# Value products in four and five matmuls, an early split of q and k, and a new order around the softmax

## The chip, the cores and the metric

One Trainium2 chip, one core of it. The metric is the device time of one execution in microseconds (us). A core's engines each work through their own queue and wait for each other by semaphores: PE (TensorE, matrix products), DVE (VectorE) and ACT (ScalarE) for elementwise work, SP and POOL, which here mostly start transfers.

## What is computed

Local and global attention (8 batches, 8 heads, 512 local and 32 global tokens, head size 64; a local query sees the local keys within 32 places and all global keys, a global query sees all keys), and a feed-forward block on the result, all in fp32:

```python
s_g = scale * np.matmul(q_g, k_all.transpose(0, 1, 3, 2))
out_g = np.matmul(sm(s_g), v_all)
s_ll = scale * np.matmul(q_l, k_l.transpose(0, 1, 3, 2))
...
s_ll = np.where(mask, s_ll, -1000000000.0)
s_lg = scale * np.matmul(q_l, k_g.transpose(0, 1, 3, 2))
s_l = np.concatenate([s_lg, s_ll], axis=-1)
a_l = sm(s_l)
out_l = np.matmul(a_l, np.concatenate([v_g, v_l], axis=2))
return np.concatenate([out_g, out_l], axis=2).astype(np.float32)
...
x = np.ascontiguousarray(attn_out.transpose(0, 2, 1, 3)).reshape(B * S, H * D)
...
h = np.maximum(x @ w_in, 0.0)
return (h * h @ w_out).astype(np.float32)
```

`sm` is the softmax with 1e-9 added to the sum; `k_all` and `v_all` are the global and the local ones together.

## The kernel before

The local tokens are cut into 16 blocks of 256, and each block with each of the 8 heads is one "head" t, 128 in all. The main loop (line 589) runs a step t for each head, with step m = t - 9 of the feed-forward block beside it (17 blocks of 256 tokens, 8 steps each: `gemm1` makes 256 hidden columns, `act1` and `act2` square the Relu and split it, `gemm2` adds to the output). The first 16 heads run in plain fp32 while the weights arrive. From then on numbers are split into a high part that PE reads fast (F32R) and a remainder, and a product is the sum of high x high, remainder x high and high x remainder. The change is about this part.

In step t, `transposes` brings the probabilities of head t-1 to the bank pt, `scores` makes those of head t, `pt_split` (ACT casts) and `pt_rest` (DVE remainders) split pt, `softmax1` to `softmax3` are the maxima (DVE), the exponentials with their sums (ACT) and the scaling by the reciprocals for two tiles of 128 queries (DVE), `av` multiplies head t-1's probabilities by its values into the bank xa, `x_evac` brings that to x_h (ACT) and x_l (DVE), which `gemm1` reads, and `split_head` splits the packed q, k and v of head t+1 (raw). The global queries ride along: `g_scores` and `g_evac` collect their scores, and per 16 heads two groups go through a table of jobs (line 654): `g_soft`, `g_exp`, `g_norm`, `g_tr` (transposes), `g_rest` (remainders), and for two pairs each `g_split_v`, `g_av` (products gxo, in the bank xa as well) and `g_x`.

From step 17 on the three engines work in the order in which the code is written (`FREE`, line 591); nothing is reordered. A tile of a pool with one buffer (xa, pt, r) is reused only when its readers are done. The profile gives nearly all instructions line 52, the helper that records them, so they are told apart by tiles.

Of the kernel before, what the change touches and what calls it, by code (L numbers as in the profile page):

```python
# [32 lines left out]
SQ = (2, 3, 4, 5, 14, 15)  # L33
# [25 lines left out]
def attention_moe(  # L59
# [65 lines left out]
    def split_head(t):  # L125

        hd = heads[t]
        raw = hd["raw"]
# [8 lines left out]
        hd["hi"], hd["lo"] = hi, lo  # L137
# [64 lines left out]
    def pt_split(t):  # L202
        hd = heads[t]
        if plain(t):
            pts = p2.tile([P, 512], F32, tag="gh", name=f"pts{t}")
            ac.copy(pts, pt)
            hd["pts"] = pts
            return
        ph = p1.tile([P, 640], F32R, tag="ph", name=f"ph{t}")
        pl = p1.tile([P, 256], F32R, tag="pl", name=f"pl{t}")  # L210
# [4 lines left out]
        hd["ph"], hd["pl"] = ph, pl  # L215

    def pt_rest(t):
        if plain(t):
            return
        ph, pl = heads[t]["ph"], heads[t]["pl"]  # L220
        ve.tensor_sub(pl, pt[:, :256], f(ph[:, :256]))
        ve.tensor_sub(ph[64:, 256:384], pt[:64, 320:448], f(ph[:64, 256:384]))

        ve.tensor_sub(ph[64:, 384:640], pt[64:, 256:512], f(ph[:64, 384:640]))

    def av(t):
        hd = heads[t]
        c = QC + KC
        if plain(t):

            xa = ps_a.tile([P, HALF], F32, tag="xa", name=f"xa{t}")
            v, pts = hd["raw"][:, c:], hd["pts"]
            mm = [
                (xa, v[:, 0:128], pts[:, 256:512]),
                (xa[:, 0:128], v[:, 64:192], pts[:, 0:128]),
                (xa[:, 128:256], v[:, 128:256], pts[:, 128:256]),
            ]
        else:
# [12 lines left out]

    def x_evac(t):
# [3 lines left out]
        if g == 0:  # L256
            ac.copy(xg[r, h // 2, :], xa)
# [7 lines left out]
    def g_load(t):  # L265
# [7 lines left out]
        if plain(t):  # L273
            qz = p1.tile([P, 512], F32, tag=("ph", "gvl", "gvh", "ph")[t // 4], name=f"qz{t}")
# [43 lines left out]
    def g_split_v(t, pair):  # L318

        gv = state["gv"]  # L320
        gvh = p1.tile([P, 5, P], F32R, tag="gvh", name=f"gvh{t}_{pair}")
        gvl = p1.tile([P, 4, P], F32R, tag="gvl", name=f"gvl{t}_{pair}")
# [3 lines left out]
        state["gvs"] = gvh, gvl  # L326
# [38 lines left out]
    def g_rest(t):  # L365
        (pth, gt), ge = state["gpt"], state["ge"]
        ptl = p1.tile([P, 512], F32R, tag="ptl", name=f"ptl{t}")
        ac.copy(pth[:64, 512:], ge[:64, :])
        ve.tensor_sub(ptl, gt, f(pth[:, :512]))
        ve.tensor_sub(pth[64:, 512:], ge[64:, :], f(pth[:64, 512:]))  # L370
        state["gpt"] = pth, ptl

    def g_av(t, pair):
        (gvh, gvl), (pth, ptl) = state["gvs"], state["gpt"]
        xo = ps_a.tile([64, P], F32, tag="xa", name=f"gxo{t}_{pair}")
        mm = []
        for c in range(4):
            cols = slice(128 * c + 64 * pair, 128 * c + 64 * pair + 64)
            mm += [(pth[:, cols], gvh[:, c, :]), (pth[:, cols], gvl[:, c, :]), (ptl[:, cols], gvh[:, c, :])]
        mm.append((pth[:, 512 + 64 * pair : 576 + 64 * pair], gvh[:, 4, :]))  # L380
        for i, (x, y) in enumerate(mm):
            pe.matmul(xo, x, y, start=i == 0, stop=i == len(mm) - 1)
        xs = p1.tile([64, P], F32, tag="xs", name=f"gxs{t}_{pair}")
        ac.activation(out=xs, in_=xo, func=AF.Copy, scale=state["gst", t][:64, pair : pair + 1])
# [58 lines left out]
    def gemm1(m, j):  # L443
# [12 lines left out]
        for n, (a, b) in enumerate(mm):  # L456
            pe.matmul(hp[:, j, :], a, b, start=n == 0, stop=n == len(mm) - 1)

    def act1(m):
# [4 lines left out]
        if m < 8 or m + LAG < NT + 8 and (m + LAG) % 16 in SQ:  # L464
# [124 lines left out]
    for t in range(NSTEP + LAG + 1):  # L589
# [53 lines left out]
        if t + 1 < NT:  # L643
            split_head(t + 1)
# [7 lines left out]
        if live and t % 4 == 3 and (t // 8) % 2 == 1:  # L652
            d = t if t % 8 == 3 else t + 2
            for at, *job in (
# [12 lines left out]
                (max(d + 6, 17), 1, g_av, 1),  # L667
                (max(d + 7, 18), 3, g_x, 1),
# [102 lines left out]
```

## Time and profile before

| | us |
|---|---|
| median of 3 runs (lowest, highest) | 1068.83 (1068.39, 1069.07) |
| the profiled execution | 1068.82 |
| its span | 1067.0 |

In the lines of the profile shown below, the engines' line gives busy time, share of the span and instructions; a line of a stretch gives, for PE, its weight loads (PEld), DVE, ACT and POOL, the busy time with the count, then the granted PE clock (1.00 is full), the DMA share and GB/s. A line of the chain has start, length and what ran; a line of a timeline has start, length, engine, operation, output and input tiles, and in brackets the idle time before it with who ended it. A group's line ends with total busy time, the mean of one in ns, and the idle time before.

### The profile page before, as it was taken

What the parts mean: (1) busy time and instruction counts of PE and PEld (TensorE: products, weight loads), DVE (VectorE), ACT (ScalarE), POOL (GpSimd) and SP (SyncE); (2) the same over time, 40 slices, a digit from 0 to 9 for tenths busy, and PEclk for the clock granted to TensorE, in tenths of its full rate; (3) what the DMA queues carried; (4) which work ended last, traced back from release to release, by engine and by line L of the source; (5) the groups of instructions that cost most, each with busy time, mean ns of one, the idle gap of its engine ahead of it and who ended that gap; (6) DMA issues with size and microseconds to landing.
All of it is one profiled execution on the core that took longest, in us unless ns stands there. A gap on an engine that the chain in (4) does not pass through costs nothing.

```text
span 1067.0 us, 21142 instructions
## 1 busy us (share of the span) xinstructions
PE 1050.4 (98%) x7568; PEld 941.7 (88%) x7568; DVE 856.3 (80%) x2687; ACT 753.1 (71%) x1901; POOL 3.9 (0%) x14
## 2 busy tenths in 40 slices
PE   7999999999999999999999999999999999999998
PEld 6776889999998989998999989999999989999896
DVE  5698988898888989988888888888888888874321
ACT  5898877778777776778777777777777787774322
POOL 1000000000000000000000000000000000000000
PEclk9999999999999999999999999999999999999999
DMA  9772132223222322222322222223221322201000
GB/s 372 310 263 74 57 106 76 71 80 98 68 89 64 103 65 83 74 91 77 94 71 82 86 72 76 90 66 100 78 89 55 94 86 66 88 29 33 13 20 20
DMA packets 54312, 96.78 MB, mean 91 GB/s; under 512 B 4288, under 2 KB 29376, under 8 KB 54208
## 3 DMA queue, kind: packets, MB, share of 16 engines
q1 hardware_dynamic: 54064, 95.37, 27.2%
q8 instruction: 60, 0.98, 0.4%
q14 instruction: 44, 0.36, 0.1%
q10 hardware_dynamic: 144, 0.07, 0.0%
HBM read 86.51 MB, written 8.91 MB: 89 GB/s over the span
## 4 chain that ended last, share of the span: by engine, by line
PE 87%; ACT 7%; DVE 4%; issue 1%; DMA 0%; ACTq 0%
PE o L52 33%; PE h L52 32%; PE xa L52 7%; PE s L52 6%; PE pt L52 5%; PE gxo L52 2%; PE gs L52 2%; ACT prob L52 1%; DVE prob L52 1%; ACT r L52 1%; ACT ph L52 1%; ACT hi L52 1%; ACT ot L52 1%; PE gt L52 1%; ACT sg L52 0%
## 5 line engine op out<-in xcount | busy, mean ns | idle before, releaser
L52 PE MATMUL h<-x_h,ws 128*128 128x256 f32 x2048 | 388.9, 283 | 0.0
L52 PEld LDWEIGHTS h<-x_h,ws 128*128 128x128 f32 x2048 | 327.0, 191 | 0.5
L52 PE MATMUL o<-ws,gh 128*128 128x512 f32 x1024 | 321.3, 395 | 0.0
L52 PE MATMUL h<-x_l,ws 128*128 128x256 f32 x1024 | 289.1, 282 | 0.1
L52 PEld LDWEIGHTS o<-ws,gh 128*128 128x128 f32 x1024 | 185.5, 188 | 34.6
L52 PE MATMUL o<-ws,gl 128*128 128x512 f32 x512 | 202.6, 396 | 0.0
L52 PEld LDWEIGHTS h<-x_l,ws 128*128 128x128 f32 x1024 | 195.9, 191 | 0.9 <-DVE x_l L52 0.4
L52 ACT CAST ph<-pt 128x256 fp32r<-128x256 f32 x448 | 141.1, 341 | 67.7 <-PE pt L52 60.8
L52 ACT ACTIVATE prob<-prob,st 128x224 f32<-128x224 f32 x270 | 127.8, 475 | 61.2 <-DVE st L52 59.1
L52 ACT ACTIVATE r<-h 128x512 f32<-128x512 f32 x136 | 81.4, 599 | 112.3 <-PE h L52 112.3
L52 PEld LDWEIGHTS o<-ws,gl 128*128 128x128 f32 x512 | 96.2, 188 | 22.7
L52 DVE CUSTOM_DVE_ANT_0 prob<-s,con 128x224 f32<-128x224 f32 x256 | 90.0, 386 | 24.5 <-PE s L52 23.2
L52 DVE TENSOR_TENSOR gl<-r,gh 128x512 fp32r<-128x512 f32 x128 | 87.9, 686 | 23.3 <-ACT gh L52 20.5
L52 ACT CAST hi<-raw 128x864 fp32r<-128x864 f32 x112 | 102.5, 915 | 1.4
L52 DVE TENSOR_TENSOR r<-h,r 128x512 f32<-128x512 f32 x82 | 56.7, 692 | 51.9 <-ACT r L52 50.6
L52 PE MATMUL xa<-ph,hi 128*64 128x128 f32 x448 | 87.3, 238 | 1.6 <-DVE ph L52 1.2
L52 DVE TENSOR_TENSOR hi<-raw,hi 64x352 fp32r<-64x352 f32 x224 | 82.5, 368 | 6.4
L52 ACT CAST gh<-r 128x512 fp32r<-128x512 f32 x128 | 79.1, 618 | 9.1 <-DVE r L52 8.7
L52 DVE TENSOR_TENSOR ph<-pt,ph 64x128 fp32r<-64x128 f32 x224 | 79.6, 355 | 7.0
L52 DVE TENSOR_TENSOR lo<-raw,hi 128x448 fp32r<-128x448 f32 x112 | 69.6, 622 | 15.3 <-ACT hi L52 12.5
L52 PE MATMUL pt<-con,prob 128*128 128x128 f32 (+1 forms) x512 | 78.2, 274 | 0.7 <-ACT prob L52 0.5
L52 DVE TENSOR_SCALAR prob<-prob,st 128x224 f32<-128x224 f32 x242 | 70.7, 334 | 4.1
(80 smaller groups left out, 1572.7 us busy)
## 6 DMA issues: line engine op xcount, KB each, us to landing
raw<-in_pk_dram SPq DMA_DIRECT2D x127, 432.0 KB, 3.2
wr<-in_w_dram SPq DMA_DIRECT2D x32, 512.0 KB, 7.9
gv<-in_vg_dram SPq DMA_DIRECT2D x32, 320.0 KB, 3.3
out_dram<-ot SPq DMA_DIRECT2D x32, 256.0 KB, 2.2
qr<-in_qg_dram SPq DMA_DIRECT2D x31, 64.0 KB, 2.8
out_dram<-ot SPq DMA_DIRECT2D x8, 64.0 KB, 1.7
con<-in_consts_dram SPq DMA_DIRECT2D x2, 224.0 KB, 5.1
raw<-in_pk_dram SPq DMA_DIRECT2D x1, 304.0 KB, 3.2
```

The lines of the kernel that those rows point to most:

```text
L52: r = method(*args, **kwargs)
```

## The change

The parts of v and of the probabilities are laid side by side, so that one product of 128 weight columns makes high x high and the remainder products at once: four matmuls for a local head instead of nine, five for a global pair instead of 13. The pieces then stand in different places of the bank, and DVE adds them (two additions more in `x_evac`, a new `g_add`). q and k get a tile of their own (kq), split before the softmax of the step before; v is split late. `pt_rest` moves ahead of the maxima. The scaling of the second tile, and Relu's square in all steps with heads, go to ACT, the global scores are scaled on ACT ahead of the transposes, and the second half of `gemm1` is cut in two around `av`. `v_g` is packed twice instead of three times, and some tiles take over others' buffers.

```diff
-        hi = p2.tile([P, PK], F32R, tag="hi", name=f"hi{t}")
-        lo = p2.tile([P, QC + 192], F32R, tag="lo", name=f"lo{t}")
-        ac.copy(hi, raw)
-        ve.tensor_sub(lo, raw[:, KC : KC + QC + 192], f(hi[:, KC : KC + QC + 192]))
...
+        kq = p2.tile([P, c + QC], F32R, tag="kq", name=f"kq{t}")
+        ac.copy(kq[:, :c], raw[:, :c])
...
+        ve.tensor_sub(hd["lo"], raw[:, KC : KC + QC], f(hi[:, KC:]))
         ve.tensor_sub(hi[64:, :KC], raw[64:, :KC], f(hi[64:, :KC]))
-        ve.tensor_sub(hi[32:64, PK - 64 :], raw[32:64, PK - 64 :], f(hi[32:64, PK - 64 :]))
...
+        ac.copy(vs[:, :, :64], vr)
+        ve.tensor_sub(vs[:, :, 64:], vr, f(vs[:, :, :64]))
...
+        for u in tiles:
-            if MUL <= t < NPLAIN:
+            if MUL <= t < NPLAIN or t >= NPLAIN and u == 1:
                 ac.activation(out=w_, in_=w_, func=AF.Copy, scale=st[:, u : u + 1])
...
-        ac.copy(ph[:, :256], pt[:, :256])
-        ac.copy(ph[:64, 256:384], pt[:64, 320:448])
-        for r in (0, 32):
-            ac.copy(ph[r : r + 32, 384:640], pt[64:96, 256:512])
+        ac.copy(pb[:, :, 0, :], pt[:, :256].rearrange("p (u n) -> p u n", u=2))
+        ac.copy(ps[:64, 512:640], pt[:64, 320:448])
+        ac.copy(ps[:64, 640:], pt[64:, 256:])
...
+            mm = [(both, vs[2], ps[:, 512:640]), (xb[:, :, 0, :], vs[3], ps[:, 640:])]
+            mm += [(xa[:, 256 * u : 256 * u + 256], vs[u], ps[:, 256 * u : 256 * u + 256]) for u in range(2)]
...
-            ac.copy(x_h[r, g % 2, h // 2, :], xa)
-            ve.tensor_sub(x_l[r, g % 2, h // 2, :], xa, f(x_h[r, g % 2, h // 2, :]))
+            ac.copy(x0, xb[:64, :, 0, :])
+            ve.tensor_sub(xr, xb[:64, :, 0, :], f(x0))
+            ve.tensor_add(xr, xb[:64, :, 1, :], xr)
+            ve.tensor_add(x1, xb[64:, :, 0, :], xr)
...
+        ac.activation(out=s[:, :544], in_=s[:, :544], func=AF.Copy, scale=st[:, 0:1])
+        for o in (544, 576):
+            ac.copy(s[:, o : o + 32], s[:, 512:544])
...
-            mm += [(pth[:, cols], gvh[:, c, :]), (pth[:, cols], gvl[:, c, :]), (ptl[:, cols], gvh[:, c, :])]
+            mm.append((xo, pts[:, o : o + 128], gvs[:, c : c + 6 : 5, :]))
...
+    def g_add(t, pair):
+        xs, xo = state["xs"]
+        ve.tensor_add(xs, xo[:64, 1, :], xs)
+        ve.tensor_add(xs, xo[64:, 0, :], xs)
...
-        if m < 8 or m + LAG < NT + 8 and (m + LAG) % 16 in SQ:
+        if m + LAG < NT:
             ac.activation(out=r, in_=r, func=AF.Square)
...
+        late, split = prev and not plain(t - 1), t + 1 < NT
         if prev:
             pt_split(t - 1)
+            if late:
+                pt_rest(t - 1)
...
+        if split and late:
+            split_kq(t + 1)
         if live:
             softmax1(t)
             softmax2(t)
-        if prev:
-            pt_rest(t - 1)
+        if split and late:
+            rest_kq(t + 1)
...
         if run:
-            gemm1(m, 1)
+            gemm1(m, 1, 0 if late else None)
+        if live and not early:
+            g_scores(t)
         if prev:
             av(t - 1)
-        if live and not early:
-            g_scores(t)
+        if run and late:
+            gemm1(m, 1, 1)
...
         if live and not early:
-            softmax3(t)
+            softmax3(t, (0,))
+        if late:
+            x_evac(t - 1)
         if run:
             act1(m)
-        if prev:
-            x_evac(t - 1)
-            if plain(t - 1):
-                w_take(-1)
+        if live and not early:
+            softmax3(t, (1,))
...
+                (d + 4, 4, g_add, 0),
...
-        for dup in range(3):
-            pk[:, hf, :, 32 * dup : 32 * dup + 32, c + 192 : c + 256] = v_g
+        for dup in range(2):
+            pk[:, hf, :, 64 * dup : 64 * dup + 32, c + 192 : c + 256] = v_g
```

Three places in the new order. The first is ACT in step 75 (head 74 is multiplied, head 75 scored), before and then after; ph and kq are the casts' outputs, r the Relu of step 66:

```order
L52 CAST ph74_7253<-pt_95 128x256 [waits PE_49,Activation_49]
L52 CAST ph74_7253<-pt_95 64x128
L52 CAST ph74_7253<-pt_95 32x256 x2
L52 ACTIVATE prob1_94,st75_7259<-prob1_94,st75_7259 128x224 [waits DVE_49]
L52 ACTIVATE prob1_94,st75_7259<-prob1_94,st75_7259 128x224
L52 ACTIVATE r66_7295<-h66_7240 128x512 [waits PE_49,Activation_49]
L52 CAST x_h_88<-xa74_7280 64x256 [waits PE_49]
L52 CAST hi76_7300<-raw76_7127 128x864 [waits DMAHW3_49]
```

```order
L51 CAST ph74_6961<-pt_95 128x2x128 [waits PE_49]
L51 CAST ph74_6961<-pt_95 64x128
L51 CAST ph74_6961<-pt_95 64x256
L51 CAST kq76_6968<-raw76_6838 128x608 [waits DMAHW3_49]
L51 ACTIVATE prob1_94,st75_6970<-prob1_94,st75_6970 128x224 [waits DVE_49]
L51 ACTIVATE prob1_94,st75_6970<-prob1_94,st75_6970 128x224
L51 CAST x_h_88<-xa74_6985 64x256 [waits PE_49]
L51 ACTIVATE r66_7004<-h66_6948 128x512 [waits PE_49,Activation_49]
L51 ACTIVATE r66_7004<-r66_7004 128x512 [waits Activation_49]
L51 ACTIVATE prob1_94<-prob1_94,st75_6970 128x224 [waits DVE_49]
L51 CAST v76_7008<-raw76_6838 128x4x64
```

The kq cast now stands between the ph casts and the exponentials, x_h ahead of Relu, and behind Relu come Square, a scaling of prob and the v cast; the gh cast follows these as before. The second is DVE in the same step, before and after; the ISA rows are the maxima, st holds them and the sums:

```order
L52 ISA prob1_94,st75_7259<-s75_7235,con_78 128x224 [waits PE_49]
L52 ISA st75_7259 128x1
L52 ISA prob1_94,st75_7259<-s75_7235,con_78 128x224
L52 ISA st75_7259 128x1
L52 TENSOR_SCALAR st75_7259<-st75_7259 128x2 [waits DVE_49]
L52 TENSOR_TENSOR pl74_7254<-pt_95,ph74_7253 128x256 [waits Activation_49]
L52 TENSOR_TENSOR ph74_7253<-pt_95,ph74_7253 64x128
L52 TENSOR_TENSOR ph74_7253<-pt_95,ph74_7253 64x256
L52 TENSOR_SCALAR st75_7259<-st75_7259 128x2 [waits Activation_49]
```

```order
L51 TENSOR_TENSOR ph74_6961<-pt_95,ph74_6961 128x2x128 [waits PE_49,Activation_49]
L51 TENSOR_TENSOR ph74_6961<-pt_95,ph74_6961 64x128
L51 TENSOR_TENSOR ph74_6961<-pt_95,ph74_6961 64x256
L51 ISA prob1_94,st75_6970<-s75_6943,con_78 128x224 [waits PE_49]
L51 ISA st75_6970 128x1
L51 ISA prob1_94,st75_6970<-s75_6943,con_78 128x224
L51 ISA st75_6970 128x1
L51 TENSOR_SCALAR st75_6970<-st75_6970 128x2 [waits DVE_49]
L51 TENSOR_TENSOR kq76_6968<-raw76_6838,kq76_6968 128x256 [waits DMAHW3_49,Activation_49]
L51 TENSOR_TENSOR kq76_6968<-raw76_6838,kq76_6968 64x352
L51 TENSOR_SCALAR st75_6970<-st75_6970 128x2 [waits Activation_49]
```

The three subtractions from pt came behind the maxima and now come ahead of them; the first waits for ACT, as it did. The third is PE at the value products (xa) of one step, before and after:

```order
L52 MATMUL xa82_8144<-ph82_8112,hi82_7936 64x128 [waits Activation_49]
L52 MATMUL xa82_8144<-ph82_8112,lo82_7937 64x128
L52 MATMUL xa82_8144<-pl82_8113,hi82_7936 64x128 [waits DVE_49]
L52 MATMUL xa82_8144<-ph82_8112,hi82_7936 64x128
L52 MATMUL xa82_8144<-ph82_8112,lo82_7937 64x128
L52 MATMUL xa82_8144<-pl82_8113,hi82_7936 64x128
L52 MATMUL xa82_8144<-ph82_8112,hi82_7936 64x128 [waits DVE_49,Activation_49]
L52 MATMUL xa82_8144<-ph82_8112,lo82_7937 64x128
L52 MATMUL xa82_8144<-ph82_8112,hi82_7936 64x256 [waits DVE_49,Activation_49]
L52 MATMUL gs82_8052<-hi83_8063,qgz_92 128x288
```

```order
L51 MATMUL h75_7877<-x_h_88,ws12_865 128x256
L51 MATMUL gs84_7920<-kq84_7788,qgz_92 128x288 [waits DVE_49]
L51 MATMUL xa83_7922<-ph83_7890,v83_7735 128x2x64
L51 MATMUL xa83_7922<-ph83_7890,v83_7735 128x2x128
L51 MATMUL xa83_7922<-ph83_7890,v83_7735 128x256 x2
L51 MATMUL h75_7877<-x_h_88,ws13_875 128x256
```

Nine products have become four, gs stands ahead of them, and six h products that stood ahead now follow. The second of the four transposes, which waited for DVE's scaling, now waits for ACT's.

More of the change, by code (lines that the diff above doesn't have):

```diff
@@ L256, in x_evac @@
         if g == 0:
-            ac.copy(xg[r, h // 2, :], xa)
-        else:
-            ac.copy(x_h[r, g % 2, h // 2, :], xa)
-            ve.tensor_sub(x_l[r, g % 2, h // 2, :], xa, f(x_h[r, g % 2, h // 2, :]))
+            ac.copy(xg[r, h // 2, :], xa[:64, :])
+            heads[t] = None
+            return
+        x0, x1 = x_h[r, g % 2, h // 2, :], x_l[r, g % 2, h // 2, :]
+        if plain(t):
+            ac.copy(x0, xa[:64, :])
+            ve.tensor_sub(x1, xa[:64, :], f(x0))
+        else:
+            xb = xa.rearrange("p (u h n) -> p u h n", u=2, h=2)
+            x0, x1 = [x.rearrange("p (u n) -> p u n", u=2) for x in (x0, x1)]
+            xr = p1.tile([P, 2, P], F32, tag="xr", name=f"xr{t}")[r]
+            ac.copy(x0, xb[:64, :, 0, :])
+            ve.tensor_sub(xr, xb[:64, :, 0, :], f(x0))
+            ve.tensor_add(xr, xb[:64, :, 1, :], xr)
+            ve.tensor_add(x1, xb[64:, :, 0, :], xr)
         heads[t] = None
@@ L325, in g_split_v @@
         ve.tensor_sub(gvh[32:64, 4, :], gv[32:64, 4, :], f(gvh[32:64, 4, :]))
-        state["gvs"] = gvh, gvl
+        state["gvs"] = gvs
     def g_soft(t):
@@ L365, in g_rest @@
     def g_rest(t):
[L366 to L371, printed above, removed]
+        (pts, pc, gc), ge = state["gpt"], state["ge"]
+        ac.copy(pts[:64, 1024:], ge[:64, :])
+        ve.tensor_sub(pc[:, :, 1, :], gc, f(pc[:, :, 0, :]))
+        ve.tensor_sub(pts[64:, 1024:], ge[64:, :], f(pts[:64, 1024:]))
     def g_av(t, pair):
-        (gvh, gvl), (pth, ptl) = state["gvs"], state["gpt"]
-        xo = ps_a.tile([64, P], F32, tag="xa", name=f"gxo{t}_{pair}")
+        gvs, pts = state["gvs"], state["gpt"][0]
+        xo = ps_a.tile([P, 2, P], F32, tag="xa", name=f"gxo{t}_{pair}")
         mm = []
         for c in range(4):
-            cols = slice(128 * c + 64 * pair, 128 * c + 64 * pair + 64)
-            mm += [(pth[:, cols], gvh[:, c, :]), (pth[:, cols], gvl[:, c, :]), (ptl[:, cols], gvh[:, c, :])]
-        mm.append((pth[:, 512 + 64 * pair : 576 + 64 * pair], gvh[:, 4, :]))
-        for i, (x, y) in enumerate(mm):
-            pe.matmul(xo, x, y, start=i == 0, stop=i == len(mm) - 1)
-        xs = p1.tile([64, P], F32, tag="xs", name=f"gxs{t}_{pair}")
-        ac.activation(out=xs, in_=xo, func=AF.Copy, scale=state["gst", t][:64, pair : pair + 1])
+            o = 256 * c + 128 * pair
+            mm.append((xo, pts[:, o : o + 128], gvs[:, c : c + 6 : 5, :]))
+        mm.append((xo[:64, 0, :], pts[:, 1024 + 64 * pair : 1088 + 64 * pair], gvs[:, 4, :]))
+        for i, (o, x, y) in enumerate(mm):
+            pe.matmul(o, x, y, start=i == 0, stop=i == len(mm) - 1, skip_group_check=True)
+        xs = p1.tile([64, P], F32, tag="xs", name=f"gxs{t}_{pair}")
+        ac.copy(xs, xo[:64, 0, :])
+        state["xs"] = xs, xo
+    def g_add(t, pair):
+        xs, xo = state["xs"]
+        ve.tensor_add(xs, xo[:64, 1, :], xs)
+        ve.tensor_add(xs, xo[64:, 0, :], xs)
         state["xs"] = xs
@@ L441, in attention_moe, with gemm1 @@
     moe = {}
-    def gemm1(m, j):
+    def gemm1(m, j, half=None):
         blk, st = divmod(m, 8)
@@ L456, in gemm1 @@
         for n, (a, b) in enumerate(mm):
-            pe.matmul(hp[:, j, :], a, b, start=n == 0, stop=n == len(mm) - 1)
+            if half in (None, 2 * n // len(mm)):
+                pe.matmul(hp[:, j, :], a, b, start=n == 0, stop=n == len(mm) - 1)
     def act1(m):
@@ L504, in evac @@
         for i in tiles:
-            pool, tag = ((p1, "ot"), (p2, "gl"))[i]
+            pool, tag = ((p1, "pth"), (p2, "gl"))[i]
             ot = pool.tile([P, DM], F32, tag=tag, name=f"ot{blk}_{i}")
@@ L632, in attention_moe @@
         if live and not early:
-            softmax3(t)
+            softmax3(t, (0,))
+        if late:
+            x_evac(t - 1)
         if run:
             act1(m)
-        if prev:
+        if live and not early:
+            softmax3(t, (1,))
+        if prev and not late:
             x_evac(t - 1)
-            if plain(t - 1):
-                w_take(-1)
+            w_take(-1)
         if early:
@@ L642, in attention_moe @@
         w_tick(t, 1)
-        if t + 1 < NT:
-            split_head(t + 1)
+        if split and not late:
+            split_kq(t + 1)
+            rest_kq(t + 1)
+        if split:
+            split_v(t + 1)
         if live:
@@ L667, in attention_moe @@
                 (max(d + 6, 17), 1, g_av, 1),
+                (max(d + 7, 18), 4, g_add, 1),
                 (max(d + 7, 18), 3, g_x, 1),
```

76 lines of the change are left out of this document (41 added, 35 removed).

## The prediction

> **What bounds the kernel now.** I read the engines' line of the page first, then the busy time in one stretch, then the chain of work that ended last, then the timelines of ScalarE (ACT), VectorE (DVE) and PE over one head.
>
> ```profile
> PE 1050.4 (98%) x7568; PEld 941.7 (88%) x7568; DVE 856.3 (80%) x2687; ACT 753.1 (71%) x1901; POOL 3.9 (0%) x14
> 500.00:600.00 100.00, 99.79 (x758) 91.26 (x757) 87.62 (x277) 73.15 (x191) 0.00 (x0) 1.00 0.25 77
> 507.59 0.78 PE gxo L52 x13
> 516.17 0.49 PE s L52 x4
> 523.50 0.44 PE s L52 x4
> 523.94 2.87 PE h L52 x24
> 526.81 0.60 PE xa L52 x9
> 527.41 0.14 PE gs L52
> 527.55 2.79 PE o L52 x12
> 530.34 0.78 PE gxo L52 x13
> 106.97 0.60 PE L52 MATMUL pt<-con,prob 128*128 128x128 f32 x4
> 508.21 0.62 PE L52 MATMUL pt<-con,prob 128*128 128x128 f32 x4
> 515.58 0.60 PE L52 MATMUL pt<-con,prob 128*128 128x128 f32 x4
> 958.13 0.60 PE L52 MATMUL pt<-con,prob 128*128 128x128 f32 x4
> ```
>
> In the stretch from 500 to 600 us PE is busy 99.79 of 100 us, and the chain there is PE alone. DVE has 87.62 and ACT 73.15, so between them they have some 12 and 27 us per 100 to give. The last two transposes rows give the length of the part that the change touches most: the four transposes of step 17 start at 106.97, those of step 128 at 958.13; that is 111 steps in 851.2 us, 7.67 us a step (a plain one 515.58 - 508.21 = 7.37, one with global work more). Before 106.97 the old order stays; after 958.13 no heads are left.
>
> That PE is full does not yet say that it stays the bound. The transposes of a step need the probabilities of that step's head, so I ask when those are ready:
>
> ```profile
> 508.87 1.29 ACT L52 CAST ph<-pt 128x256 fp32r<-128x256 f32 x4
> 510.33 0.48 ACT L52 ACTIVATE prob<-prob,st 128x224 f32<-128x224 f32 x1 [0.17 <-DVE st L52]
> 510.72 0.18 ACT L52 ACTIVATION_READ_ACCUMULATOR prob<-prob,st 128x1 f32 x1
> 510.81 0.47 ACT L52 ACTIVATE prob<-prob,st 128x224 f32<-128x224 f32 x1
> 511.19 0.18 ACT L52 ACTIVATION_READ_ACCUMULATOR prob<-prob,st 128x1 f32 x1
> 512.30 0.60 ACT L52 ACTIVATE r<-h 128x512 f32<-128x512 f32 x1 [0.93 <-PE h L52]
> 512.93 0.63 ACT L52 ACTIVATE r<-r 128x512 f32<-128x512 f32 x1
> 513.47 0.35 ACT L52 CAST x_h<-xa 64x256 fp32r<-64x256 f32 x1
> 513.72 0.91 ACT L52 CAST hi<-raw 128x864 fp32r<-128x864 f32 x1
> 514.66 0.40 ACT L52 COPY sg<-gs 64x288 f32<-64x288 f32 x1
> 514.96 0.62 ACT L52 CAST gh<-r 128x512 fp32r<-128x512 f32 x1
> 509.39 0.38 DVE L52 CUSTOM_DVE_ANT_0 prob<-s,con 128x224 f32<-128x224 f32 x1
> 510.12 0.17 DVE L52 TENSOR_SCALAR st<-st 128x2 f32<-128x2 f32 x1
> 510.20 0.42 DVE L52 TENSOR_TENSOR pl<-pt,ph 128x256 fp32r<-128x256 f32 x1
> 510.65 0.74 DVE L52 TENSOR_TENSOR ph<-pt,ph 64x128 fp32r<-64x128 f32 x2
> 512.71 0.58 DVE L52 TENSOR_SCALAR prob<-prob,st 128x224 f32<-128x224 f32 x2
> 513.85 0.42 DVE L52 TENSOR_TENSOR x_l<-xa,x_h 64x256 fp32r<-64x256 f32 x1 [0.56 <-ACT x_h L52]
> ```
>
> The step's transposes started at 508.21. The first exponential starts 2.1 us later (510.33), because the maxima need only the scores; both scalings end at 512.71 + 0.58 = 513.29, and PE asks for them at 515.58. So the softmax has 2.3 us to spare, and PE never waits.
>
> **The change on PE.** The nine value products take 0.60 us: eight of 128 columns at 0.06 and one of 256 at 0.12 (the 24 h products of 256 columns take 2.87, 0.12 each). After it there are three of 256 (0.36) and one of 128 columns with a 128-wide weight. That one isn't in the trace: 0.06 is its lower bound (a 64-wide weight), 0.12 the upper (256 columns behind a 128-wide weight); the nearest row, four s products behind 128-wide weights in 0.44, says 0.11, which I take. Sum 0.47, a gain of 0.13 on each of 112 heads, 14.6 us. The Trainium skill ("TensorE: Matmul & The Clock Gate", Part 2) lets the load's time grow with the weight's columns, and its Part 1 puts products at N / 2.4 GHz + 2.5 ns; by that alone the small product would be 0.056 us and the heads would save 6 us more in all, but the s rows here lie above it. The global products go from 0.78 to 4 x 0.12 + 0.06 = 0.54 us: 0.24 x 32 = 7.7 us. Cutting gemm1 in two, and moving the value products between, costs PE nothing. **PE saves 22.3 us**, and a plain step needs 2.87 + 2.79 + 0.44 (pt) + 0.44 + 0.14 + 0.47 = 7.15 us of it.
>
> **The change on ACT and DVE: a ring.** In the new order the DVE remainders of the previous head's probabilities stand ahead of this head's maxima, and they wait for the last of the three ACT casts. The second half's scaling is ACT's now, behind x_h, Relu and Square, and the transposes wait for it. Both engines work in the order written, so one step closes on itself: casts, remainders, maxima, exponentials, x_h, Relu, Square, scaling, v cast, gh cast, next casts. Further rows for its terms:
>
> ```profile
> L52 ACT CAST ph<-pt 32x256 fp32r<-32x256 f32 x224 | 82.0, 366 | 4.1
> L52 ACT CAST gvh<-gv 128x640 fp32r<-128x640 f32 x32 | 23.0, 718 | 0.0
> L52 ACT COPY ot<-o 128x512 f32<-128x512 f32 x34 | 18.5, 589 | 3.6 <-PE o L52 3.0
> L52 ACT ACTIVATE sg<-sg,gst 128x544 f32<-128x544 f32 x16 | 11.9, 746 | 0.0
> L52 ACT CAST pth<-gt 128x512 fp32r<-128x512 f32 x16 | 9.4, 587 | 11.7 <-PE gt L52 11.7
> L52 ACT CAST qgz<-qr 128x128 fp32r<-128x128 f32 x28 | 8.4, 299 | 0.7
> L52 ACT CAST pth<-gs 64x128 fp32r<-64x128 f32 x16 | 4.2, 260 | 0.3
> L52 DVE TENSOR_TENSOR ptl<-gt,pth 128x512 fp32r<-128x512 f32 x16 | 11.0, 687 | 2.2 <-ACT pth L52 1.4
> L52 DVE TENSOR_TENSOR pth<-gs,pth 64x128 fp32r<-64x128 f32 x16 | 4.7, 294 | 7.1 <-ACT pth L52 7.0
> ```
>
> Instructions of one engine that don't depend on each other overlap by about 0.1 us (sg ends at 515.06, gh starts at 514.96); a hand-over costs 0.03 to 0.04 (513.82 to 513.85). The ring, in us:
> - three casts instead of four: 1.29 - 0.37 = 0.92; hand-over 0.03
> - remainders, 510.20 to 511.39: 1.19; gap 0.03
> - maxima, 509.39 to 510.29: 0.90; hand-over 0.04
> - both exponentials, 510.33 to 511.37: 1.04
> - x_h 0.35 and a gap of 0.02
> - Relu and Square, 512.30 to 513.56: 1.26, and 0.03 ahead
> - the scaling. The ACT rows of prob are 0.47 to 0.48 long; less the overlap 0.38
> - v, 128x256: by the casts of 512 (0.62) and 864 columns (0.91) an estimate of 0.41, less overlap 0.31
> - gh 0.62 less overlap 0.52
>
> That is **7.02 us**, about PE's 7.15; no spare time is left. The strided forms (2x128, 4x64) aren't in the trace: below stand the contiguous rows, above the same in two pieces (two 64x128 casts of 0.26 less an overlap, 0.42 for 0.37), so 0.15 a step for the three in the ring; I take the contiguous rows, which have the same columns. The kq cast (about 0.70 by the same two rows) hides in ACT's wait for remainders and maxima; without it ACT would merely idle. The kq remainders hide behind the exponentials, the three x additions (3 x 0.42, dependent) behind Square, scaling and casts; if that cover fails they delay only the xa bank (below).
>
> So whatever else ACT does in a step now lengthens it. Per 16 heads:
> - ACT, as before: eight sg evacuations at 0.42 (hi to gh with one between, against without), 3.4; four qgz at 0.33, 1.3; four ot copies at 0.49, 2.0; four gvh at 0.63, 2.5; two pth at 0.49, 1.0; two sg exponentials with their read, 1.5; four gxs at 0.26 (as the 64x128 cast), 1.0. Sum 12.7.
> - ACT, new: scaling the global scores and two 32-column copies. Not in the trace; below by nothing, if a wait covers them, above by two 0.75 rows each; the 128x544 row is nearest, and with two short copies I take 1.1, twice, 2.2.
> - DVE, between remainders and maxima: the global remainders 0.69 + 0.29 + 0.03, twice, 2.0; the new g_add, two dependent additions of 64x128 (0.29 each, with gaps 0.63), four times, 2.5.
> - one bank, xa, serves the value products and the global ones. In the two steps with global remainders and a gv split, DVE's queue from the casts' start on is 2.1 (casts, remainders), 1.0 (global), 0.9 (maxima), 1.0 (kq), 1.9 (wait for gvh and two gv subtractions, by the 0.69 and 0.29 rows), 0.8 (reciprocal and scaling), 1.3 (three additions): 8.9 us. gxo waits for that, and its 0.54 stands ahead of the transposes, which the ring would release at 7.02 + 1.64 - 0.8 = 7.9; less the gh cast, which runs beside, the next casts start some 1.2 late. Twice, 2.4.
>
> Together 21.8 per 16 heads, 1.36 a step; two steps in 16 carry none and take PE's 7.15, 0.02 a step more. The step is 7.02 + 1.36 + 0.02 = **8.40 us against 7.67**. Over 111 steps that is 81 us. The profiled execution took 1068.82 us (span 1067.0), the same as the median 1068.83: **1150 us**. Square on ACT (0.63, in 65 more steps) and DVE's freed multiplication are in the ring already. The new packing of v_g, the renamed buffers and the early part's changes cost nothing: their transfers land many us ahead of use.
>
> **The rivals.**
> - *PE stays the bound.* The mechanism: the distance from casts to exponentials overlaps instead of adding up, for instance because the first remainder runs beside the second and third cast. Place: the wait of the exponentials for DVE. Price: none, so PE's gain shows, 1068.8 - 22.3 = 1046.5. It decides once the mean ring, extras included, is below PE's 7.47 us (7.67 - 0.20); my ring must be 0.9 too long. Against it: DVE's first remainder waits for the third cast. The Trainium skill's "Perfetto Trace Analysis" ("Identifying the Most-Contended Engine") would bet on this one: work taken off the engine with the highest occupancy, PE's 98% here, is what helps. The 2.3 us of spare time that the change spends stands in no occupancy row. 10%.
> - *Only ACT's extras count*, DVE's 4.5 and the bank's 2.4 are hidden: 7.02 + 14.9 / 16 = 7.95, 31 us more, 1100. 12%.
> - *DVE becomes the bound too*: three dependent additions and later gl push remainders behind; another 0.3 a step gives 1183 and more. 6%.
> - *It cancels*: about half of the extras is hidden and the step stays near 7.67 (within 0.2%, about what a measurement of this kernel can tell from no change). 2%.
>
> **How the numbers follow.** My forecast holds 70%, its own range 1115 to 1183 (0.15 us on the ring and 0.15 on the extras, each way, times 111). Taking in the ACT-only case and the lower edge of the DVE case, the range is 1100 to 1183. Slower 0.88, same 0.02, faster 0.10.
>
> **What would show it.** Right: PE busy near 90% of the span, its idle time ahead of pt, released by ACT's prob; ACT waiting about 1.5 us a step for DVE's st, and no longer for h or pt; value products 0.47 us, gxo 0.54. Wrong: PE at 98% and steps of 7.47; or ACT's exponentials starting within 3 us of the transposes, where I say 4.

## The result, and the profile after

| | us | ratio to before, 95% |
|---|---|---|
| before, median | 1068.83 (1068.39 to 1069.07) | |
| changed, median | 1157.55 (1157.54 to 1157.87) | 1.0832 [1.0814, 1.0851] |
| changed, profiled execution | 1157.87, span 1156.1 | |

The change makes the kernel 88.7 us slower, close to the 1150 forecast. The first lines are from the page of the changed kernel (engines, and engines of the chain that ended last), the third from its windows (start:end, length, busy us of PE, PEld, DVE, ACT, POOL), the rest from its PE timeline (start, duration):

```profile
PE 1057.7 (91%) x6752; PEld 923.0 (80%) x6752; DVE 895.9 (77%) x2750; ACT 809.5 (70%) x2126; POOL 3.9 (0%) x14
ACT 41%; DVE 33%; PE 20%; issue 6%; DMA 1%; ACTq 0%; DVEq 0%
500.00:600.00 100.00, 91.86 (x611) 81.36 (x609) 83.45 (x262) 73.42 (x196) 0.00 (x0) 1.00 0.25 77
106.31 0.60 PE L51 MATMUL pt<-con,prob 128*128 128x128 f32 x4
583.80 0.60 PE L51 MATMUL pt<-con,prob 128*128 128x128 f32 x4
590.95 0.60 PE L51 MATMUL pt<-con,prob 128*128 128x128 f32 x4
599.63 0.60 PE L51 MATMUL pt<-con,prob 128*128 128x128 f32 x4
1047.17 0.60 PE L51 MATMUL pt<-con,prob 128*128 128x128 f32 x4
```

No engine is full any more (PE, the nearest, is at 91%), yet the kernel is slower: the chain, which was PE's for 87% before, now alternates between ACT, DVE and PE. The first and the last transposes row span the same 111 steps as before: 940.86 us against 851.2, or 8.48 a step against 7.67. That is 89.7 us, so all of the loss lies there; the stretches ahead and behind are as long as they were. PE's need in a step is as forecast: from 583.80 to 590.95, 7.15 us, it does a plain step without a pause. The next step takes 8.68.

The steps are far from equal. This table, worked out from the starts of the transposes, lines up 16 steps (one round of the global work, somewhere between 480 and 750 us) of six kernels; the experiments below are named as there.

| step | before | changed | E3 | E9 | E11 | E12 |
|---|---|---|---|---|---|---|
| 1 | 7.28 | 8.97 | 7.19 | 7.16 | 7.27 | 7.16 |
| 2 | 8.12 | 8.91 | 8.96 | 9.08 | 8.17 | 8.74 |
| 3 | 8.62 | 11.32 | 9.93 | 9.92 | 8.90 | 9.56 |
| 4 | 7.37 | 7.57 | 7.20 | 7.18 | 7.59 | 7.18 |
| 5 | 7.32 | 7.25 | 7.54 | 7.14 | 7.32 | 7.16 |
| 6 | 8.06 | 8.61 | 8.02 | 7.93 | 7.81 | 8.10 |
| 7 | 7.28 | 7.84 | 7.20 | 7.16 | 7.28 | 7.17 |
| 8 | 7.30 | 7.15 | 7.30 | 7.18 | 7.44 | 7.16 |
| 9 | 7.27 | 8.68 | 7.16 | 7.14 | 7.27 | 7.15 |
| 10 | 7.29 | 7.13 | 7.15 | 7.66 | 7.29 | 7.16 |
| 11 | 7.27 | 7.42 | 7.16 | 7.15 | 7.27 | 7.15 |
| 12 | 7.95 | 9.33 | 8.09 | 8.56 | 7.73 | 7.88 |
| 13 | 8.63 | 11.03 | 9.64 | 9.63 | 8.38 | 9.54 |
| 14 | 7.36 | 7.58 | 7.19 | 7.15 | 7.59 | 7.17 |
| 15 | 7.33 | 7.60 | 7.92 | 7.36 | 7.34 | 7.35 |
| 16 | 8.05 | 8.61 | 8.02 | 8.10 | 7.81 | 8.28 |
| sum | 122.5 | 135.0 | 125.7 | 125.5 | 122.5 | 123.9 |

Past the first round most cells come again within 0.03 us in the rounds that follow, but not all: in the kernel before, step 12 took 7.95 in this round and 7.71 to 7.73 in the others, where the sum is 122.3; step 10 of E3 and E9 and step 12 of E9 change from round to round, by up to 1.1. Products gxo run in steps 3, 6, 13 and 16, the transposes gt of the global scores in steps 2 and 12.

The waits of the changed kernel (engine and tile, what ended the wait; us, times, longest):

```profile
ACT prob L51 <- DVE st L51: 218.0, 121, 4.5
ACT r L51 <- PE h L51: 51.4, 21, 3.8
PE gxo L51 <- DVE x_l L51: 22.2, 15, 2.1
PE o L51 <- ACT ot L51: 16.4, 14, 1.2
PE gt L51 <- DVE x_l L51: 13.7, 13, 1.1
PE gs L51 <- DVE pth L51: 11.1, 13, 1.1
PE xa L51 <- DVE gxs L51: 7.2, 27, 0.5
ACT ph L51 <- PE pt L51: 5.3, 23, 0.9
```

ACT's waits for PE's h and pt were 112.3 us in 103 times and 60.8 in 67; they are down to 51.4 in 21 and 5.3 in 23. Its wait for DVE's st grew from 59.1 to 218.0, the mark that the prediction named. The PE rows tell where PE itself stands idle: ahead of gxo and gt, which share the bank xa with the value products and wait for DVE's x_l, and ahead of o, gs and xa. Ahead of the transposes pt it waits 0.3 us in the whole execution; the prediction had looked for its idle time there. One closing of the ring stands in the timelines of ACT and DVE, here over a step with a gvh cast in it (the second exponential, x_h and the reads between are left out):

```profile
561.12 0.92 ACT L51 CAST ph<-pt 128x256 fp32r<-128x256 f32 x3
561.94 0.70 ACT L51 CAST kq<-raw 128x608 fp32r<-128x608 f32 x1
562.07 1.18 DVE L51 TENSOR_TENSOR ph<-pt,ph 128x256 fp32r<-128x256 f32 x3
563.28 0.39 DVE L51 CUSTOM_DVE_ANT_0 prob<-s,con 128x224 f32<-128x224 f32 x1
564.03 0.17 DVE L51 TENSOR_SCALAR st<-st 128x2 f32<-128x2 f32 x1
564.23 0.48 ACT L51 ACTIVATE prob<-prob,st 128x224 f32<-128x224 f32 x1 [1.59 <-DVE st L51]
565.68 0.60 ACT L51 ACTIVATE r<-h 128x512 f32<-128x512 f32 x1
566.31 0.63 ACT L51 ACTIVATE r<-r 128x512 f32<-128x512 f32 x1
566.85 0.47 ACT L51 ACTIVATE prob<-prob,st 128x224 f32<-128x224 f32 x1
567.22 0.39 ACT L51 CAST v<-raw 128x256 fp32r<-128x256 f32 x1
567.52 0.72 ACT L51 CAST gvh<-gv 128x640 fp32r<-128x640 f32 x1
568.15 0.61 ACT L51 CAST gh<-r 128x512 fp32r<-128x512 f32 x1
568.67 0.92 ACT L51 CAST ph<-pt 128x256 fp32r<-128x256 f32 x3
```

Follow it: casts at 561.12, remainders when the casts end, maxima behind them, the exponential 1.59 us late, then every ACT instruction back to back until the next casts at 568.67. That is 7.55 us; without the gvh cast, 0.63, it is 6.92, where the sum of the prediction was 7.02. (Behind 568.67 this step goes another way: the next remainders start only at 570.00, 0.41 after the last cast, since gvh's subtraction and gl stand ahead of them in DVE's queue. In three steps of 16 the chain reaches the remainders that way, through DVE, and not through the casts.)

### The profile page after: what moved, and what is told of

Read it like the earlier page. It is cut to its first block, busy times and chain, and to the rows that moved or that the text cites. A ratio compares the mean times of both kernels' runs of the same rounds, so it can differ in the third digit from the quotient of the medians.

```text
span 1156.1 us, 19674 instructions
## 1 busy us (share of the span) xinstructions
PE 1057.7 (91%) x6752; PEld 923.0 (80%) x6752; DVE 895.9 (77%) x2750; ACT 809.5 (70%) x2126; POOL 3.9 (0%) x14
## 3 DMA queue, kind: packets, MB, share of 16 engines
HBM read 86.51 MB, written 8.91 MB: 83 GB/s over the span
## 4 chain that ended last, share of the span: by engine, by line
ACT 41%; DVE 33%; PE 20%; issue 6%; DMA 1%; ACTq 0%; DVEq 0%
DVE ph L51 11%; ACT prob L51 9%; ACT r L51 8%; PE o L51 8%; DVE prob L51 7%; ACT ph L51 7%; PE h L51 6%; ACT sg L51 4%; ACT gh L51 3%; ACT x_h L51 3%; DVE st L51 3%; ACT v L51 2%; DVE gvh L51 2%; DVE kq L51 2%; DVE xr L51 2%
## 5 line engine op out<-in xcount | busy, mean ns | idle before, releaser
L51 PE MATMUL h<-x_h,ws 128*128 128x256 f32 x2048 | 406.4, 283 | 0.0
L51 PE MATMUL o<-ws,gh 128*128 128x512 f32 x1024 | 323.2, 397 | 16.4 <-ACT ot L51 16.4
L51 ACT ACTIVATE prob<-prob,st 128x224 f32<-128x224 f32 x382 | 180.0, 473 | 218.1 <-DVE st L51 218.0
L51 DVE TENSOR_TENSOR ph<-pt,ph 128x256 fp32r<-128x256 f32 x336 | 127.2, 379 | 58.3 <-ACT ph L51 53.1
L51 ACT ACTIVATE r<-h 128x512 f32<-128x512 f32 x136 | 81.0, 595 | 52.7 <-PE h L51 51.4
L51 DVE TENSOR_TENSOR kq<-raw,kq 128x256 fp32r<-128x256 f32 x224 | 106.1, 474 | 1.9 <-issue 0.3
L51 ACT CAST ph<-pt 128x256 fp32r<-128x256 f32 x336 | 100.1, 333 | 8.6 <-PE pt L51 5.3
L51 DVE CUSTOM_DVE_ANT_0 prob<-s,con 128x224 f32<-128x224 f32 x256 | 90.6, 389 | 17.3 <-PE s L51 13.2
L51 PE MATMUL xa<-ph,v 128*128 128x128 f32 x448 | 82.8, 292 | 15.5 <-DVE ph L51 7.5
L51 PEld LDWEIGHTS xa<-ph,v 128*128 128x128 f32 x448 | 63.9, 189 | 29.0 <-issue 27.0
L51 ACT CAST kq<-raw 128x608 fp32r<-128x608 f32 x112 | 78.3, 699 | 3.6 <-DMA raw<-in_pk_dram 3.6
L51 ACT ACTIVATE r<-r 128x512 f32<-128x512 f32 x119 | 75.2, 632 | 3.6
L51 PE MATMUL s<-kq 128*128 128x224 f32 x448 | 77.2, 294 | 0.0
```

The source lines that it names most:

```text
L51: r = method(*args, **kwargs)
```

## Experiments

The theory is the prediction's: the new order closes a ring through ACT and DVE, and only what stands on it costs time. The main rivals: ACT and DVE simply have more to do; or the bank xa sets the long steps. The mean step named with each run is the distance from the first to the last of the 111 transposes, divided by 111.

### Load or place: the same needless copies in two places (E4, E5)

Two copies of 160 columns each are added to ACT in every step: in E4 where it waits for the maxima, in E5 between x_h and Relu, on the ring.

```diff
+    spare = cp.tile([P, 160], F32, name="spare")
 E4, behind split_kq(t + 1):        E5, behind x_evac(t - 1), ahead of act1(m):
+        if late and live:
+            for _ in range(2):
+                ac.copy(spare, con[:, :160])
```

> Two needless ACT copies (128x160, about 0.53 us together) in each step with split heads, between the kq cast and the exponentials, where ACT waits some 1.5 us for DVE's maxima; all else as in the changed kernel. Ring theory: they lie beside the ring, no change, 1152 to 1163 us. Rival, ACT's load as such sets the time: 111 x 0.53 = 59 us more, 1216 us.

> The same two copies, but between x_h and Relu, on the ring. Ring theory: nearly all of 59 us more, less what other loops of about the same length hide (0.13 us in a plain step): 1195 to 1217 us. Rival, DVE or PE sets the time: 1157 to 1170 us.

E4: **1157.08 us**, 1.0824 [1.0803, 1.0846], mean step 8.48. E5: **1213.00 us**, 1.1348 [1.1325, 1.1370], mean step 8.98. ACT's timeline, first two rows of E4, then two of E5:

```profile
601.69 0.68 ACT L51 COPY spare<-con 128x160 f32<-128x160 f32 x2
603.38 0.48 ACT L51 ACTIVATE prob<-prob,st 128x224 f32<-128x224 f32 x1 [1.00 <-DVE st L51]
```

```profile
601.19 0.68 ACT L51 COPY spare<-con 128x160 f32<-128x160 f32 x2
601.78 0.59 ACT L51 ACTIVATE r<-h 128x512 f32<-128x512 f32 x1
```

In E4 the copies eat into a wait, and 1.00 us of it is still left; in E5 Relu starts right behind them, 0.59 us after they began. The same work costs nothing in one place and 55.5 us, 0.50 a step, in the other. The rival by load falls; the ring stands.

### Undoing the order: remainders behind the maxima (E1), the second scaling on DVE (E2), both (E3)

```diff
 E1
             pt_split(t - 1)
-            if late:
-                pt_rest(t - 1)
...
             softmax2(t)
+        if late:
+            pt_rest(t - 1)
 E2
-            if MUL <= t < NPLAIN or t >= NPLAIN and u == 1:
+            if MUL <= t < NPLAIN:
...
-            softmax3(t, (0,))
+            softmax3(t)
...
-        if live and not early:
-            softmax3(t, (1,))
```

> The remainders of the probabilities go back behind the maxima (and stand ahead of the kq remainders); the rest of the change stays. Ring theory: the exponentials no longer wait for 1.19 us of remainders nor for the last ph cast, so the ring falls from 7.02 to about 5.5 us plus some 1.2 of extras, below what PE needs; PE becomes the bound again, with some stalls at the value products: steps of 7.45 to 7.9 us instead of 8.48, 1045 to 1095 us in all. Rival, DVE and ACT are simply overloaded (their work is unchanged here): 1140 us or more.

> The scaling of the second tile goes back to DVE; the rest of the change stays. Ring theory: the ring stays closed by the order of ACT (gh cast, then the next casts) and only loses the scaling's 0.38 us: about 42 us less than the changed kernel, 1115 us (1105 to 1130). Rival, the transposes' wait for ACT's late scaling is what holds PE: without it Relu, Square and scaling leave the path and PE is the bound again, below 1070 us. Rival, DVE is the bound: no gain, 1155 us or more.

> Both edits: remainders behind the maxima, both scalings on DVE; the products in four and five, the split of q and k, Square on ACT and the additions stay. Ring theory: ring near 5.2 us plus extras, DVE busy about 7 us a step; PE is the bound and its saving shows: 1046 to 1075 us, so about the time before or up to 2% faster. Rival, the new products themselves are slower on PE than counted, or DVE is overloaded: 1090 us or more.

E1: **1100.87 us**, 1.0298 [1.0277, 1.0318], mean step 7.96. E2: **1151.42**, 1.0770 [1.0749, 1.0792], 8.41. E3: **1097.22**, 1.0271 [1.0254, 1.0288], 7.93.

E1 ends a little above the range that the ring gave, but takes back 56.7 of the 88.7 us by one moved call, and ACT's wait for st falls from 218.0 to 37.0 us: the remainders ahead of the maxima are the costly part of the new order. E2 is a miss: the scaling stands on ACT for 0.38 us a step, and taking it off should have given most of 42 us, but gives 6, nearly the "no gain" of its second rival. The chain of waits shows why; first a step of the changed kernel (the view ends at 600, which cuts its last row), then the like step in E2 (start, us, engine and tile):

```profile
596.09 0.59 ACT ot L51
596.73 3.06 PE o L51 x12
599.79 0.22 PE pt L51 x2
```

```profile
593.00 0.59 ACT ot L51
593.64 3.06 PE o L51 x12
596.71 0.45 PE pt L51 x4
```

The transposes at the end of this step don't wait for the scaling. gemm2's products (o) wait for ACT to copy the outputs of the group before (ot), and the transposes come behind them; this is so in two steps of 16. In other steps gxo waits for DVE's x_l, or PE is simply full, or the loop is DVE's: there both scalings (0.58 us a step, against 0.34 for the one in the changed kernel) stand ahead of the additions, gl and the next remainders, and the chain comes to the remainders that way in five steps of 16 instead of three. Where the ring closed last, the step shortens (step 12 from 9.33 to 8.85, step 2 from 8.91 to 8.55), and the next loop, a little shorter, takes over. E3 then misses too, by more than 20 us, and lies where its rival (DVE overloaded, 1090 us or more) had it; the ring is open (ACT waits 35.4 us for st), but its window shows DVE busy for 91 of 100 us, and in the table its plain steps are short and steps 2, 3, 12 and 13 long:

```profile
500.00:600.00 100.00, 96.45 (x642) 86.00 (x641) 90.97 (x287) 74.73 (x200) 0.00 (x0) 1.00 0.25 76
```

### The bank and the order on PE (E6, E7, E9)

E6 moves the two subtractions for gv of pair 0, which stand ahead of the x additions in DVE's queue, to the step's end. E7 is E3 with this, with g_scores behind the value products, and g_add behind the maxima. E9 is E3 with gemm1's second half in one piece and the value products ahead of g_scores.

```diff
 E6
+    def g_sub_v(t, pair):
+        gv, gvs = state["gv"], state["gvs"]
...
...
                 (d + 3, 3, g_split_v, 0),
+                (d + 3, 2, g_sub_v, 0),
 E7, on E3 and E6
...
-                (d + 4, 4, g_add, 0),
+                (d + 4, 3, g_add, 0),
 E9, on E3
-            gemm1(m, 1, 0 if late else None)
-        if live and not early:
-            g_scores(t)
+            gemm1(m, 1)
         if prev:
             av(t - 1)
-        if run and late:
-            gemm1(m, 1, 1)
+        if live and not early:
+            g_scores(t)
```

> In the two steps of 16 heads that split the first pair of global values, DVE does these two subtractions behind the three x additions instead of ahead of the reciprocals; all else as in the changed kernel. If the bank xa is what makes these steps 11.0 and 11.3 us long, the global products start about 0.95 us earlier: 14 x 0.95 = 13 us less, 1144 us (1138 to 1151). If not: 1157 us.

> Remainders behind the maxima and both scalings on DVE (as in the run with both edits, 1097.2 us), and the late gv subtractions, the global scores behind the value products, and the two global additions behind the maxima. If what was left over PE's own need in that run are waits for the banks xa and gs, most of them go: 1070 to 1088 us. If DVE's load (about 7 us a step) is what is left: 1093 us or more. To beat the kernel before it would have to come below 1067.

> The run with both edits (1097.2 us), and PE's old order: the second half of gemm1 in one piece, then the value products, then the global scores. If the value products' waits for the remainders and the global scores' wait are what kept that run above PE's own need, they are gone: 1070 to 1085 us. If the bank xa and DVE's three additions behind it are, the products come 0.7 us later and so do the additions: 1097 us or more.

E6: **1163.29 us**, 1.0883 [1.0861, 1.0904], mean step 8.52. E7: **1136.84**, 1.0634 [1.0616, 1.0652], 8.29. E9: **1090.07**, 1.0196 [1.0177, 1.0215], 7.87.

E6 was to gain 13 us and lost 6. Three rows of its chain, then three of E7's:

```profile
635.74 0.43 DVE v L51
636.17 0.61 DVE gvh L51
636.91 0.77 PE gxo L51 x5
```

```profile
628.19 0.29 DVE gxs L51
628.50 0.30 DVE gxs L51
628.94 0.70 PE xa L51 x4
```

In E6 gxo no longer waits for x_l but for the moved subtractions, which now stand behind the remainder of v: the wait has only changed its name (25.5 us in 14 waits for gvh, where it was 22.2 in 15 for x_l). So E6 does not tell what the bank alone costs. In E7 the next head's value products wait for the late g_add, which holds the bank xa (45.0 us in 28 waits, 7.2 in 27 in the changed kernel), so the early place of g_add is right. E7 changes the place of g_scores and of the gv subtractions too, but its loss on E3, 39.6 us, is about what this one wait grew by. E9, between the two expectations, gains 7 us on E3: PE's order matters a little. A plain step there takes PE's 7.15, and what is long beyond the kernel before is steps 2, 3, 12 and 13.

### The products without the order, and each half alone (E10, E11, E12)

E10 keeps the new products and additions but goes back to the old order, and to Relu's square on ACT in six steps of 16 only, on DVE in the others. E11 is the kernel before with the global half alone (nine-fold packing, scaling ahead of the transposes, additions). E12 is E9 with the old global half, so the local half alone, in the best order found.

```diff
 E10, on E9
-        if m + LAG < NT:
+        if m < 8 or m + LAG < NT + 8 and (m + LAG) % 16 in (2, 3, 4, 5, 14, 15):
...
-        if late:
-            x_evac(t - 1)
         if run:
             act1(m)
-        if prev and not late:
+        if prev:
             x_evac(t - 1)
...
-        if split and not late:
+        if split:
             split_kq(t + 1)
             rest_kq(t + 1)
 E11, on the kernel before (E12, on E9, is this backwards)
-            mm += [(pth[:, cols], gvh[:, c, :]), (pth[:, cols], gvl[:, c, :]), (ptl[:, cols], gvh[:, c, :])]
...
+            mm.append((xo, pts[:, o : o + 128], gvs[:, c : c + 6 : 5, :]))
...
+    def g_add(t, pair):
```

> The products alone: four and five matmuls with the additions and the new global scaling that they need, but the old order, q and k split at the end of a step, both scalings on DVE, Square on ACT in six steps of 16 only. The ring is open here, PE saves 22 us, and DVE has 0.9 us a step more (subtractions and additions of 0.42 each, five of them for three older ones) and g_add. If DVE's load decides, its 6.7 us a step become 7.7 and more with waits: 1080 to 1110 us. If PE still decides, 1046 to 1055 us.

> The kernel before with the global half of the change alone: global products in five matmuls, their additions, the global scores scaled on ACT; local heads as before. PE saves 0.24 x 32 = 7.7 us, DVE has some 0.1 us a step more. If PE stays the bound, 1061 to 1066 us, faster than both kernels; if the two additions hold the bank xa, 1068 to 1080 us.

> The run with PE's old order (1090.1 us), and the global half as in the kernel before: 13 products, no g_add, the global scores scaled behind the product. PE has 7.7 us more, DVE some 15 us less in all. If DVE's queue and the bank xa in the steps with global work hold that run, 1070 to 1083 us; if PE does, 1095 us or more.

E10: **1139.35 us**, 1.0657 [1.0637, 1.0677], mean step 8.32. E11: **1070.35**, 1.0011 [1.0002, 1.0020], 7.69. E12: **1082.95**, 1.0129 [1.0113, 1.0146], 7.80. The windows of E10, then of E12:

```profile
500.00:600.00 100.00, 94.10 (x624) 83.52 (x624) 91.18 (x283) 65.58 (x178) 0.00 (x0) 1.00 0.25 78
```

```profile
500.00:600.00 100.00, 97.14 (x678) 87.72 (x678) 91.08 (x294) 72.51 (x196) 0.00 (x0) 1.00 0.25 76
```

E10 was expected at 1080 to 1110 with DVE as the bound, or at 1046 to 1055; it takes more than either. In the old order the additions stand ahead of the kq remainders in DVE's queue, the scores wait for those (23.5 us in 34 waits), and the chain of the whole execution is 53% DVE. So the new order isn't idle: given the new products, what E9 keeps of it (q and k split early, the x additions ahead of Relu, Square on ACT) wins back 49 us (E10 to E9; which of the three does it was not tried apart). But the products have made the need for it.

E11 shows that the global half's saving on PE is real and is spent at once: of the four steps with gxo, 6, 13 and 16 are 0.24 to 0.25 shorter, as gxo's 0.24 asks, steps 3, 4, 8 and 14 are 0.14 to 0.28 longer, and the sum is about the same (122.5 against the usual 122.3; step 12's 0.22 is only the odd value before). In step 3 PE now waits 0.70 for DVE's sg ahead of gs, a wait that wasn't there; the other three steps were not followed.

E12 is the plainest, at the upper end of the 1070 to 1083 that it should take if DVE's queue and the bank xa hold it. Its plain steps take 7.15 to 7.18 against 7.27 to 7.30: the 0.13 us of the value products show fully. But steps 3 and 13 take 9.56 and 9.54 against 8.62 and 8.63. PE and DVE rows at the end of such a step, before, and then in E12:

```profile
506.87 0.42 DVE L52 TENSOR_TENSOR x_l<-xa,x_h 64x256 fp32r<-64x256 f32 x1
507.43 0.22 PE L52 MATMUL gxo<-gvh,pth 128*64 128x128 f32 x1
```

```profile
514.60 0.42 DVE L51 TENSOR_TENSOR xr<-xa,x_h 64x256 f32<-64x256 f32 x1
515.05 0.42 DVE L51 TENSOR_TENSOR xr<-xa,xr 64x256 f32<-64x256 f32 x1
515.50 0.43 DVE L51 TENSOR_TENSOR x_l<-xa,xr 64x256 fp32r<-64x256 f32 x1
516.08 0.24 PE L51 MATMUL gxo<-gvh,pth 128*64 128x128 f32 x1 [0.86 <-DVE x_l L51]
```

Before, x_l ended at 507.29 and gxo, which takes the same bank, started 0.14 later without a wait; 0.15 is what the hand-over takes in E12 (515.93 to 516.08), so there was no spare time at all. In E12 two more additions of 0.45 each, start to start, stand ahead of x_l, and gxo waits 0.86. The steps grow by 0.91 to 0.94, just the two additions. Step 2 goes the same way: there gt, in the same bank, waits 0.57 for x_l, and the step grows by 0.62. This is read from the trace, not tried by a kernel with a second bank.

### The local half with the second scaling on ACT, early (E13)

```diff
 E13, on E12: the second tile's scaling on ACT, between x_h and Relu
-            if MUL <= t < NPLAIN:
+            if MUL <= t < NPLAIN or t >= NPLAIN and u == 1:
...
-            softmax3(t)
+            softmax3(t, (0,))
         if late:
             x_evac(t - 1)
+        if live and not early:
+            softmax3(t, (1,))
         if run:
             act1(m)
```

> The same, and the second tile's scaling on ACT, right behind x_h and ahead of Relu, so that the transposes don't wait for Relu and Square. DVE has 0.25 us a step less, ACT 0.38 more of its spare 25%. If DVE's queue still sets the step, 5 to 15 us below the run beside it, 1060 to 1075 us, perhaps below the kernel before; if ACT's order now closes a ring, above it.

**1099.54 us**, 1.0287 [1.0272, 1.0302], mean step 7.95: not the gain that was hoped for but the other case named, a ring closed by ACT's order. DVE's busy time falls from 903.8 us in E12 to 889.1, and the kernel is 16.6 us slower. ACT's waits in E12 and in E13:

```profile
ACT prob L51 <- DVE st L51: 42.8, 61, 4.4
```

```profile
ACT prob L51 <- DVE st L51: 109.4, 143, 4.4
```

The scaling needs DVE's reciprocal. Put ahead of Relu it makes ACT stand still until that comes (1.44 us at 505.47), and Relu, Square and gh behind it are late. In a plain step this costs nothing (7.15 us, as in E12); in the steps with global work, where DVE comes late, the chain runs through scaling, Relu, Square, v and gh on ACT to gl and the next maxima on DVE (there from 505.47 to 508.65), and steps 3, 6, 12, 13, 15 and 16 are 0.2 to 0.5 longer. DVE's load went down, the kernel got slower: place again, not load. None of these versions beats the kernel before.

## Why the prediction was right

- **PE's need** (22.3 us less, 7.15 us in a plain step): right. 7.15 was measured from 583.80 to 590.95; the four value products in it take 0.47 (586.97 to 587.44), as summed with 0.11 for the small one; E12's plain steps are 0.13 shorter than before, three of E11's four steps with gxo 0.24.
- **The ring** (7.02 us): right, 6.92. Term by term in the rows at 561 to 568.67, from start to start where they overlap: casts 0.92, remainders 1.18, from the first exponential to Relu 1.45 (forecast 1.44), Relu and Square 1.26, the scaling 0.37, v 0.30, gh 0.52. E4 and E5 show that it is place on this ring that costs. This is one step's ring; three steps of 16 close through DVE's queue instead, as said above.
- **The kq cast costs nothing**: right. In the rows at 561.94 it lies in ACT's wait, and E4 put 0.68 us more into it for nothing.
- **The extras** (21.8 us per 16 steps, a mean step of 8.40): the mean was 8.48; 940.86 us against 111 x 8.40 = 932.4 is 8.5, which is the 7.6 by which 1150 fell short and a little more. What the steps have above 7.15 is 135.0 - 16 x 7.15 = 20.6 in the table, where the forecast had 16 x 8.40 - 16 x 7.15 = 20.0. The sum was right; its spread was not foreseen. The two steps with the global remainders and a gv split (3 and 13 in the table) carry 8.05 of it, the plain ones nothing. That the sum came so near is in part luck, since the terms were not all right: PE's wait at gxo was 1.5 us each (22.2 in 15), where the forecast had the casts 1.2 late, and with the ot copies the way goes on through 3.1 us of o on PE, not through the scaling and gh, as the sum has it. Something else must have come out smaller; which, the runs don't show. (The seven stretches of DVE's queue in that term add up to 9.0, not 8.9; twice in 16 steps, this is 1.4 us of the time.)
- **The scaling as a term of its own** (0.38 us, every step): the size is right, but what it is worth when taken away is not (E2: 6 us, not 42). A sum of a ring's terms tells how long the ring is, not what each term would bring, since loops of almost its length stand behind it.
- **PE's idle time ahead of pt, released by ACT's prob**: wrong. The prediction had the transposes wait for ACT's late scaling; PE hardly did (0.3 us ahead of pt in the whole execution). PE stands idle at gxo, o, gt, gs and xa (22.2, 16.4, 13.7, 11.1 and 14.7 us), that is, for the bank xa, for copies and for remainders. The scaling counts by its place in ACT's queue, not by what waits for it.
- **Loops that the prediction lacked**: gemm2 waits for the ot copies (16.4 us on PE). The copies were in the sum as ACT's extras, 2.0 per 16 steps, but not as something that PE waits for. The other goes round in DVE's queue, through the additions and gl to the next remainders (three steps of 16, five in E2).
- **The rivals.** *PE stays the bound* fell: 8.48 a step, not 7.47. The Trainium skill ("Perfetto Trace Analysis", "Identifying the Most-Contended Engine") says to optimize the engine with the highest occupancy first, and to judge TensorE's headroom by its weight loads' busy share instead; by either, 98% or 88%, that was PE. Work was taken off it, and the kernel is 88.7 us slower with PE at 91%. *Only ACT's extras count* (1100) and *it cancels* fell as well. *DVE is the bound too* did not hold for the changed kernel, with DVE at 83.45 of 100 us, but is what stands behind the ring: with the ring open (E3, E9, E12) DVE has 91 of 100, and the additions on x cost in the steps with global work more than PE saves (E12).

What stays open: how far a second bank for the global products would bring E12 down. Its steps 3 and 13 are together 1.85 us longer than before and its 16 steps together 1.4 (1.6 against the usual round), so this would decide the sign; but E6 shows that another wait may stand right behind.

## What to carry to other kernels

Where several engines work in the written order, look for the closed loops (who waits for whom, around to the same instruction of the next step) and add up their lengths; busy shares don't show them, and the same 0.5 us of work cost nothing inside a wait and 55.5 us on the loop. Before work is moved off the busiest engine onto another, look at the tightest step rather than the mean: DVE had 12 us in 100 to spare, and none on the way of one bank through its queue in two steps of 16. An edit that undoes one term of a loop gives only the distance to the next loop.

## What was not expected of the hardware

PE's busy time did not tell what its work had become. Some 22 us of products were taken off, and the page has 1057.7 us busy against 1050.4 before. Rows of the groups (count, busy us, mean ns of one), of the changed kernel and of E9, where gemm1 is again in one piece:

```profile
L51 PE MATMUL h<-x_h,ws 128*128 128x256 f32 x2048 | 406.4, 283 | 0.0
```

```profile
L51 PE MATMUL h<-x_h,ws 128*128 128x256 f32 x2048 | 389.1, 283 | 0.0
```

The same 2048 products of the same 283 ns count 17.3 us more where the run of them is cut in two, since a record lasts 0.28 us while the next product starts 0.12 later: each break in the run shows the end of one record more, by 0.16 us, and 112 breaks, one a head, would be 17.9 us. Distances from start to start, as in the 7.15 us above, are free of this.
